# A 256-byte tile for a one-column constant: where the operands of the feed-forward matmuls begin

## The chip, the cores and the metric

The kernel runs on one core of a Trainium2 chip. The metric is the device time of one execution in microseconds (us), median of three runs. Beside the timed runs there is one profiled execution of the kernel; all rows shown here are of that one.

## What is computed

The input is q, k, v of 2 x 8 heads, 768 tokens, head size 64, and two pairs of weights, 512 x 2048 and 2048 x 512. Everything is float32 (the weights arrive as the bits of float64).

```python
# attention, per head: a window of +-15 tokens, and block summaries of 32 tokens
k_sum, v_sum = max over each block of k, mean over each block of v
scores = [q k^T / 8 in the window, q k_sum^T / 8 + log(32)]
x = softmax(scores) @ [v, v_sum]              # -> 1536 tokens x 512
# first network
h = x @ w_in;  g = h - tanh(h);               x = g @ w_out
# second network
h = x @ w_in2; g = h * tanh(softplus(h));     out = g @ w_out2
```

## The kernel before

**Stages.** The attention comes first (some 87 us, units of 128 tokens, loads of keys `kt`, queries `qz` and values beside it), then the two networks. In the last steps of the attention the first blocks of the first network already run.

**The networks.** The 1536 tokens are cut into 3 chunks of 512, d_ff into 16 slices of 128; a step is one network f, one chunk c, one slice i, and there are 2 x 3 x 16 = 96 steps. `ffn_in` (line 489) computes the hidden slice h of a step: 4 pieces of the 512 model columns, each in three matmuls by `mm3` (lines 485 to 487), 12 matmuls of 128 x 128 weights and 512 moving columns. `ffn_out` (line 557) multiplies the gated slice by the slice's output weights into 4 accumulators (`x`, `x`, `tr`, `tr`), again 4 times three matmuls. Three, because every float32 is held as a high and a low part (`xhi`, `xlo`; `ghi`, `glo`; `w[:, 0]`, `w[:, 1]`): high by high, high by low, low by high.

**Operands.** `mm3(out, w, x)` takes `w` as the stationary operand, which a separate load of weights brings in, and `x` as the moving one. In `ffn_in` the weights are a piece of `W[i]` and the moving operand is `xhi` or `xlo`. In `ffn_out` the weights are a piece of `W[i]` and the moving operand is `ghi` or `glo` for the first network (f = 0); for the second (f = 1) `lhs, rhs = (w, g) if f == 0 else (g, w)` exchanges the two. In the rows below the moving operand is named first: `xhi,w`, `ghi,w` and `w,ghi`.

**Order.** It is written out by hand (`tc.manual_schedule()`, the loop from line 628 on): at step n the in-block of step n + 2 is issued, then the out-block of step n - 2. So TensorE's queue holds blocks of 12 matmuls, in and out by turns, with an out-block four slices behind the in-block in front of it; at the end five out-blocks follow one another. Between the two stand the gates: ScalarE and VectorE turn h into `t`, then `ghi` and `glo` (`g_hi`, `g_lo`, lines 503 to 510, two buffers each). The second network's gate takes logarithms, `gate_2n` (line 531), and adds 2 there by a bias column:

```python
    two_c = big.tile([128, 1], F32, name="two_c")             # line 74
        nc.scalar.activation(out=r, in_=n, func=ACTF.Ln, bias=two_c)   # line 537
```

**The weights** are converted from the bits of float64 to the two float32 parts beside everything else, by ScalarE and VectorE (`conv_top`, `conv_or`, `conv_hi`, `conv_lo`), with loads through SyncE's queue.

**Where tiles lie.** Tiles of a pool stand one behind the other in each partition of the on-chip memory, and pools one behind the other, from the left or, with `side="right"`, from the right end. A tile's size is rounded up to 32 bytes. In bytes from the partition's start:

| Tiles | pool | begin at | modulo 256 |
|---|---|---|---|
| xhi0 to xhi2, xlo0 to xlo2, 8192 each | big | 16,512 to 57,472 | 128 |
| w0, w1, w2, 8192 each | big | 65,664, 73,856, 82,048 | 128 |
| two_c, 4 (takes 32) | big | 90,240 | 128 |
| t, ghi, glo, two buffers of 2048 each | tmp | 90,272 to 100,512 | 160 |
| kt0 to kt7, 3328 each; qz0 to qz2, 4096 each | kq (attention only) | 102,560 to 137,376 | 160 |
| w3 to w6, later w7 to w15, 8192 each | wb3, wb7 (kq's place and above) | 102,560 to 200,864 | 160 |

w15 ends at 209,056; on the right, the values, masks, identity and staging buffers begin at fixed places that don't depend on the left side. Within these tiles the operands of the feed-forward matmuls begin at multiples of 512 bytes (weights) or 2048 bytes (moving operand).

Of the kernel before, what the change touches and what calls it, by code (L numbers as in the profile page):

```python
# [9 lines left out]
F32 = mybir.dt.float32  # L10
# [16 lines left out]
def kernel(  # L27
# [7 lines left out]
    w2_d: bass.AP,  # L35
    out: bass.AP,
):
    """qt_d [unit, (e d), hp, 128]: q transposed, head = 2 * hp + e; a unit is 128 tokens.
    kw_d [unit, (e d), hp, 160]: a unit's keys and 16 on either side, transposed; 0 outside the
    sequence.  # L40
    vw_d [unit, 2, 96, h, d]: the values of each half of a unit and 16 on either side.
    vt_d [batch, group, (e d), hp, 256]: v transposed.
    w1_d, w2_d [d_ff / 128, 128, 1024]: the bits of float64 weights, w_in's and w_out's part
    of one slice of d_ff side by side."""
    nc = tc.nc
    NU, _, HP, _ = qt_d.shape
    B, NG = vt_d.shape[:2]
# [15 lines left out]
    big = ctx.enter_context(tc.tile_pool(name="big", bufs=1))  # L63
# [7 lines left out]
    xlo = [big.tile([128, KD, CH], F32R, name=f"xlo{c}") for c in range(NC)]  # L71
    W = {i: big.tile([128, 2, 1024], F32R, name=f"w{i}") for i in range(NPRE)}

    two_c = big.tile([128, 1], F32, name="two_c")
    nc.gpsimd.memset(two_c, 2.0)

    def pst(tag):
        return ps.tile([128, 512], F32, tag=tag, name=tag)

    # The bits of a float64 -> a float32 (its first 24 bits) -> the two float32r parts of that.  # L80
    # The upper 16 bits of a float64, read as a bfloat16 and turned into a float16, are the upper
    # 16 bits of the float32: their exponents' low 3 bits lie in the mantissa, and what lies above
    # loses 112 of its offset, 8 * 112 = 1023 - 127. The middle 32 bits give the rest of the mantissa;
    # they are a word of their own, as the loads land 2 bytes early.
    PW = 256
    IN, OUT = range(0, DM, PW), range(DM, 1024, PW)
    pieces = []
# [6 lines left out]
    def top_tiles(n):  # L94
        tiles = [stg.tile([128, PW], I32, name=f"top{i}") for i in range(n)]
        for t in tiles:
            nc.gpsimd.memset(t, 0)
        return tiles

    def free(n):  # L100
        f, i, o = pieces[n]
        return i in W if f == 0 else (n_in, n_out)[o >= DM] > steps.index((0, NC - 1, i))
# [9 lines left out]
    def conv_top(n):  # L112
        nc.scalar.activation(  # L113
            out=tops[n % len(tops)].bitcast(F16).rearrange("p (n t) -> p n t", t=2)[:, :, 1],
            in_=raws[n].bitcast(BF16).rearrange("p (n t) -> p n t", t=4)[:, :, 2], func=ACTF.Copy,
        )

    def conv_or(n):
        tmps[n] = stg.tile([128, PW], I32, tag="cv", name="cv", bufs=n_cv)
        nc.vector.scalar_tensor_tensor(  # L120
            out=tmps[n], in0=raws.pop(n).bitcast(I32).rearrange("p (n t) -> p n t", t=2)[:, :, 0],
            scalar=13, in1=tops[n % len(tops)], op0=ALU.logical_shift_right, op1=ALU.bitwise_or,
        )

    def conv_hi(n, on_pool):
        f, i, o = pieces[n]
        hi, t = W[i][:, 0, o:o + PW], tmps[n].bitcast(F32)
        if on_pool:
            nc.gpsimd.tensor_copy(hi, t)
        else:  # L130
            nc.scalar.activation(out=hi, in_=t, func=ACTF.Copy)  # L131

    def conv_lo(n, on_pool=False):
        f, i, o = pieces[n]
        ready.add(pieces[n])
        (nc.gpsimd if on_pool else nc.vector).tensor_tensor(  # L136
            out=W[i][:, 1, o:o + PW], in0=tmps.pop(n).bitcast(F32),
            in1=W[i][:, 0, o:o + PW].bitcast(F32), op=ALU.subtract,
        )
# [3 lines left out]
    def conv_ahead(end):  # L143
        nonlocal nl
        while nl < min(n1 + n_raw, end):
            conv_load(nl)
            nl += 1

    def conv_tick(limit, hi_pool=False, lo_pool=False):
        """The first steps of one piece, the middle ones of the one before, the last one of the  # L150
        one before that."""
        nonlocal n0, n1, n2, n3
        while n0 < min(limit, n1 + 2):
            conv_ahead(n0 + 1)
            conv_top(n0)
            n0 += 1
        if n1 < min(n0, n3 + n_cv):
            conv_or(n1)
            n1 += 1
        conv_ahead(limit)  # L160
        if n3 < n2:
            conv_lo(n3, lo_pool)
            n3 += 1
        if n2 < n1 and free(n2):
            conv_hi(n2, hi_pool)
            n2 += 1

    # What shares the attention's work among the engines, by step of the loop below (a step is one
    # unit and parity of heads), or by unit for FILL_DVE
    ASB_DVE = (0, 2, 7, 11, 12, 13, 14, 15, 17, 20, 21)  # L170
    NORM_DVE = (0, 13, 21, 23)
    FILL_DVE = (0, 1, 4, 5, 6, 7, 8, 9, 11)
# [5 lines left out]
    def attention(actx):  # L178
        con = actx.enter_context(tc.tile_pool(name="con", bufs=1, side="right"))
        two = actx.enter_context(tc.tile_pool(name="two", bufs=2, side="right"))  # L180
# [20 lines left out]
        def constants():  # L201
            nonlocal tops
            make_identity(nc, ident)
            k_edges(0)
            for m in range(3):
                nc.gpsimd.memset(masks[m], 0.0)
                for s in range(2):
                    rows = masks[m][T * s:T * s + T]
                    nc.gpsimd.memset(rows[:, SUM[s][0]:SUM[s][1]], math.sqrt(D) * math.log(BLK))
                    reg = rows[:, WND[s][0]:WND[s][1]]  # L210
                    # kept where 1 <= j - i <= 31, and where the key is in the sequence
                    conds = [([[1, KW]], -1, -1), ([[-1, KW]], 2 * WIN - 1, 1)]
                    if (m, s) == (0, 0):
                        conds.append(([[1, KW]], -WIN, 0))
                    if (m, s) == (2, 1):
                        conds.append(([[-1, KW]], KW - WIN - 1, 0))
                    for pattern, base, mul in conds:
                        nc.gpsimd.affine_select(
                            out=reg, in_=reg, pattern=pattern, base=base, channel_multiplier=mul,
                            compare_op=ALU.is_ge, fill=-BIG,  # L220
                        )
            k_edges(UPB)
            tops = top_tiles(2)
# [9 lines left out]
            )  # L233

        def k_edges(u):
            """The 16 keys on either side of the border in front of unit u."""
            l, r = NB, NB + WIN + 128
            if 0 < u < UPB:
                nc.scalar.copy(kt[u][:, :, l:l + WIN], kt[u - 1][:, :, r - WIN:r])
                nc.scalar.copy(kt[u - 1][:, :, r:r + WIN], kt[u][:, :, l + WIN:l + 2 * WIN])  # L240
            elif u == 0:
                nc.gpsimd.memset(kt[0][:, :, l:l + WIN], 0.0)
            else:
                nc.gpsimd.memset(kt[UPB - 1][:, :, r:r + WIN], 0.0)
# [155 lines left out]
        for n in range(3):  # L400
            q_zero(n)
        constants()
        warm = pst("x")
        for n in range(NWARM):
            nc.tensor.matmul(out=warm[:, 0:128], lhsT=ident, rhs=ident, start=n == 0, stop=n == NWARM - 1)
        for u in range(UPB):
            k_sum(u)
            if u:
                k_edges(u)
# [32 lines left out]
        def ticks(j, counts):  # L442
            for _ in range(counts.get(j, 0)):
                conv_tick(len(pieces) // 2, j in HI_POOL, j in LO_POOL)
# [74 lines left out]
        g_hi(z, ts[z])  # L519
        g_lo(z, ts.pop(z))  # L520

    # tanh(softplus(h)) = n / (n + 2), n = u (u + 2), u = exp(min(h, 20)); the reciprocal is
    # exp(-ln(n + 2)) and a Newton step
    def gate_2u(z):
        t = ts[z] = tmp.tile([128, CH], F32, tag="t", name="t")
        nc.scalar.activation(out=t, in_=hs[z], func=ACTF.Exp)
# [63 lines left out]
    steps = [(f, c, i) for f in range(2) for c in range(NC) for i in range(NI)]  # L590
# [31 lines left out]
    with tc.manual_schedule():  # L622
# [5 lines left out]
        for n in range(NS + 2):  # L628
# [17 lines left out]
            if f == 0:  # L646
                more_out(n - 2)
                evac()
                if n == N2 - 1:
                    go(N2, gate_2e)  # L650
                if n:
                    g_hi(z, ts[z])
                if n < N2 - 2:
                    conv_tick(limit)
                if n:
                    g_lo(z, ts.pop(z))
                if n == N2 - 1:
                    go(N2, gate_2f)
                if n < N2 - 2:
                    conv_tick(limit)  # L660
                if n and n + 1 < N2:
                    gate_1(steps[n + 1])
                if n == N2 - 2:
                    nc.scalar.preload_act_table_set("natural_log_exp_and_others")
                    go(N2, gate_2u, gate_2m, gate_2n)
                if n < N2 - 2:
                    conv_tick(limit)
                    conv_tick(limit)
                if n == N2 - 1:
                    go(N2 + 1, gate_2u, gate_2m)  # L670
                continue
# [93 lines left out]
```

## Time and profile before

| | |
|---|---|
| three runs | 619.6, 620.08, 621.63 us; median 620.08 |
| profiled execution: span from the first to the last instruction | 619.7 us |
| TensorE busy (matmul) | 603.5 us, 3212 matmuls |
| VectorE, ScalarE, GpSimd busy | 421.3, 330.4, 53.3 us |
| TensorE's granted clock, mean | 0.997 |

Beside the span the profile gives no further time of that execution. PE is TensorE's matmuls, PEld its loads of weights, DVE VectorE, ACT ScalarE, POOL GpSimd, SP SyncE. Times in rows are in us from the span's start. Matmuls are pipelined: a row's duration (0.39 us) overlaps the next row's, so the distance between two starts tells the pace.

### The profile page before, as it was taken

The numbers are of one execution on the slowest core, as the hardware profiler recorded it, in microseconds if no ns is written. First come the engines' busy times: TensorE is split into PE (matmuls) and PEld (weight loads), VectorE is DVE, ScalarE is ACT, GpSimd is POOL, SyncE is SP. The second block draws the span as 40 slices with busy tenths as digits, with TensorE's granted clock in tenths as the row PEclk, the third lists the DMA queues.
The fourth block names the chain that finished last, engine by engine and source line by source line (L and its number), as shares of the span: only waits on it lengthen the run. The fifth ranks groups of instructions, "written<-read, shape, count | busy, mean of one in ns | idle before, by whom it ended". The sixth has DMA issues, their size and how long they took to land.

```text
span 619.7 us, 9228 instructions
## 1 busy us (share of the span) xinstructions
PE 603.5 (97%) x3212; PEld 493.5 (80%) x3212; DVE 421.3 (68%) x972; ACT 330.4 (53%) x793; POOL 53.3 (9%) x109
## 2 busy tenths in 40 slices
PE   6798999999999999999999999999999999999997
PEld 6587888888888888888888888888888888888886
DVE  6777968877242222367777479997778777597785
ACT  4687868877252112356766456654454444454442
POOL 5545651000000000000000000000000000000000
PEclk9899999999999999999999999999999999999999
DMA  9999547666120000135662101200010000100001
GB/s 232 237 264 255 160 124 249 218 202 190 33 69 17 1 0 1 34 100 150 193 189 68 51 1 51 64 7 1 7 62 1 1 1 0 69 1 1 1 1 68
DMA packets 32302, 52.20 MB, mean 84 GB/s; under 512 B 3392, under 2 KB 25920, under 8 KB 32256
## 3 DMA queue, kind: packets, MB, share of 16 engines
q1 hardware_dynamic: 32256, 51.62, 28.8%
q8 instruction: 25, 0.41, 0.3%
q14 instruction: 21, 0.17, 0.1%
HBM read 48.07 MB, written 3.15 MB: 83 GB/s over the span
## 4 chain that ended last, share of the span: by engine, by line
PE 92%; DMA 6%; SPq 1%; POOL 0%; issue 0%; DVE 0%; POOLq 0%
PE aT L485 7%; PE s L485 7%; PE aT L486 7%; PE s L486 7%; PE aT L487 7%; PE x L485 7%; PE s L487 7%; PE x L486 7%; PE x L487 7%; PE tr L487 7%; PE tr L485 7%; PE tr L486 7%; PE x L368 3%; DMA vtc<-in_vt_dram 2%; PE aT L354 1%; DMA qz<-in_qt_dram 1%
## 5 line engine op out<-in xcount | busy, mean ns | idle before, releaser
L510 DVE TENSOR_TENSOR glo<-t,ghi 128x512 fp32r<-128x512 f32 x48 | 33.4, 696 | 92.3 <-ACT ghi L505 92.2
L505 ACT ACTIVATE ghi<-t 128x512 fp32r<-128x512 f32 x48 | 30.3, 630 | 102.6 <-PE tr L487 102.6
L485 PE MATMUL aT<-xhi,w 128*128 128x512 f32 x192 | 76.1, 396 | 0.0
L485 PE MATMUL s<-xhi,w 128*128 128x512 f32 x192 | 76.0, 396 | 0.0
L486 PE MATMUL aT<-xlo,w 128*128 128x512 f32 x192 | 75.9, 395 | 0.0
L487 PE MATMUL aT<-xhi,w 128*128 128x512 f32 x192 | 75.8, 395 | 0.0
L486 PE MATMUL s<-xlo,w 128*128 128x512 f32 x192 | 75.8, 395 | 0.0
L487 PE MATMUL s<-xhi,w 128*128 128x512 f32 x192 | 75.7, 394 | 0.0
L113 ACT ACTIVATE top<-raw 128x256 f16<-128x256 bf16 x128 | 61.7, 488 | 12.6 <-ACT w L131 5.3
L120 DVE SCALAR_TENSOR_TENSOR cv<-raw,top 128x256 int32<-128x256 int32 x128 | 55.4, 434 | 10.8 <-ACT top L113 7.2
L131 ACT ACTIVATE w<-cv 128x256 fp32r<-128x256 f32 x120 | 47.4, 401 | 9.8 <-DVE cv L120 8.8
L136 DVE TENSOR_TENSOR w<-cv,w 128x256 fp32r<-128x256 f32 x114 | 48.3, 425 | 0.2 <-ACT w L131 0.2
L541 DVE SCALAR_TENSOR_TENSOR t<-n,r 128x512 f32<-128x512 f32 x48 | 33.1, 691 | 20.2 <-ACT r L538 20.1
L510 DVE TENSOR_TENSOR glo<-n,ghi 128x512 fp32r<-128x512 f32 x48 | 33.1, 689 | 16.8 <-ACT ghi L505 16.8
L334 ACT ACTIVATE aa<-aa,neg 128x120 f32<-128x120 f32 x96 | 36.6, 383 | 14.2 <-DVE neg L329 14.2
L505 ACT ACTIVATE ghi<-n 128x512 fp32r<-128x512 f32 x48 | 30.3, 631 | 25.9 <-PE tr L486 18.3
L487 PEld LDWEIGHTS aT<-xhi,w 128*128 128x128 f32 x192 | 36.1, 188 | 8.7
L487 PEld LDWEIGHTS s<-xhi,w 128*128 128x128 f32 x192 | 36.1, 188 | 8.6
L485 PEld LDWEIGHTS aT<-xhi,w 128*128 128x128 f32 x192 | 36.0, 188 | 8.5
L485 PEld LDWEIGHTS s<-xhi,w 128*128 128x128 f32 x192 | 36.0, 188 | 8.5
L486 PEld LDWEIGHTS aT<-xlo,w 128*128 128x128 f32 x192 | 36.1, 188 | 8.3
L486 PEld LDWEIGHTS s<-xlo,w 128*128 128x128 f32 x192 | 36.1, 188 | 8.3
(99 smaller groups left out, 1308.7 us busy)
## 6 DMA issues: line engine op xcount, KB each, us to landing
raw<-in_w_dram SPq DMA_DIRECT2D x128, 255.8 KB, 3.6
vu<-in_vw_dram SPq DMA_DIRECT2D x24, 192.0 KB, 5.9
qz<-in_qt_dram SPq DMA_DIRECT2D x24, 128.0 KB, 6.6
vtc<-in_vt_dram SPq DMA_DIRECT2D x6, 512.0 KB, 7.1
out_dram<-o SPq DMA_DIRECT2D x9, 256.0 KB, 2.1
kt<-in_kw_dram SPq DMA_DIRECT2D x6, 320.0 KB, 5.3
kt<-in_kw_dram SPq DMA_DIRECT2D x6, 256.0 KB, 4.8
out_dram<-t SPq DMA_DIRECT2D x3, 256.0 KB, 2.1
```

Of the source, the lines that this page charges most:

```text
L113: nc.scalar.activation(out=tops[n % len(tops)].bitcast(F16).rearrange("p (n t) -> p n t", t=2)[:, :, 1], in_=raws[n].bitcast(BF16).rearran ...
L120: nc.vector.scalar_tensor_tensor(out=tmps[n], in0=raws.pop(n).bitcast(I32).rearrange("p (n t) -> p n t", t=2)[:, :, 0], scalar=13, in1=top ...
L131: nc.scalar.activation(out=hi, in_=t, func=ACTF.Copy)
L136: (nc.gpsimd if on_pool else nc.vector).tensor_tensor(out=W[i][:, 1, o:o + PW], in0=tmps.pop(n).bitcast(F32), in1=W[i][:, 0, o:o + PW].bit ...
L334: nc.scalar.activation(out=aa[u][:, e, hp, :], in_=aa[u][:, e, hp, :], func=ACTF.Exp, scale=-1.0, bias=neg[u][:, e, hp:hp + 1], accum_out= ...
L368: nc.tensor.matmul(out=xps[u][64 * e:64 * e + 64, hp, T * s:T * s + T], lhsT=vu[u % 3][:, s, 2 * hp + e, :], rhs=asb[u, e][:, hp, T * s:T ...
L485: nc.tensor.matmul(out=out, lhsT=w[0], rhs=x[0], start=first, stop=False)
L486: nc.tensor.matmul(out=out, lhsT=w[0], rhs=x[1], start=False, stop=False)
L487: nc.tensor.matmul(out=out, lhsT=w[1], rhs=x[0], start=False, stop=last)
L505: nc.scalar.activation(out=ghi, in_=t, func=ACTF.Copy)
L510: nc.vector.tensor_tensor(out=glo, in0=t, in1=ghi.bitcast(F32), op=ALU.subtract)
L541: nc.vector.scalar_tensor_tensor(out=ts[z], in0=ns[z], scalar=2.0, in1=rs[z], op0=ALU.add, op1=ALU.mult)
```

## The change

The constant's tile gets 64 columns, of which the first is used. The rest of the diff takes out comments and a docstring and leaves their lines empty, so line numbers stay.

```diff
-    two_c = big.tile([128, 1], F32, name="two_c")
+
+    two_c = big.tile([128, 64], F32, name="two_c")[:, 0:1]
     nc.gpsimd.memset(two_c, 2.0)
```

The tile takes 256 bytes, so what stands behind it on the left begins 224 bytes further on.

## Rows read from the trace of the kernel before

**Rows 1.** The page: busy time, share of the span and instructions of each engine.
```profile
PE 603.5 (97%) x3212; PEld 493.5 (80%) x3212; DVE 421.3 (68%) x972; ACT 330.4 (53%) x793; POOL 53.3 (9%) x109
```

**Rows 2.** The page: chain that ended last, share of the span by engine.
```profile
PE 92%; DMA 6%; SPq 1%; POOL 0%; issue 0%; DVE 0%; POOLq 0%
```

**Rows 3.** Waits of TensorE, whole span: us in total, times, longest (first, last of six).
```profile
PE s L314 <- DMA qz<-in_qt_dram: 5.7, 3, 2.8
...
PE tr L293 <- DVE vsum L280: 0.4, 1, 0.4
```

**Rows 4.** Windows: stretch, us, busy of each engine (instructions), clock, DMA share, GB/s.
```profile
0.00:60.00 60.00, 47.66 (x598) 41.24 (x599) 43.30 (x212) 41.98 (x175) 31.64 (x79) 0.97 0.99 250
97.00:602.11 505.11, 505.11 (x2186) 410.13 (x2185) 337.74 (x648) 254.55 (x517) 0.56 (x2) 1.00 0.20 60
349.50:602.00 252.50, 252.50 (x1093) 205.03 (x1092) 199.80 (x345) 126.61 (x215) 0.00 (x0) 1.00 0.05 16
```

**Rows 5.** Timeline of TensorE, first network: start, duration, line, out<-operands; first matmuls of blocks.
```profile
87.29 0.50 PE L485 MATMUL aT<-xhi,w 128*128 128x512 f32 x1
...
160.93 0.39 PE L485 MATMUL s<-xhi,w 128*128 128x512 f32 x1
...
163.68 0.39 PE L485 MATMUL x<-ghi,w 128*128 128x512 f32 x1
...
171.94 0.39 PE L485 MATMUL aT<-xhi,w 128*128 128x512 f32 x1
...
173.10 0.39 PE L487 MATMUL aT<-xhi,w 128*128 128x512 f32 x1
...
174.46 0.40 PE L487 MATMUL aT<-xhi,w 128*128 128x512 f32 x1
...
182.98 0.40 PE L485 MATMUL s<-xhi,w 128*128 128x512 f32 x1
...
185.79 0.39 PE L485 MATMUL x<-ghi,w 128*128 128x512 f32 x1
...
188.58 0.40 PE L485 MATMUL s<-xhi,w 128*128 128x512 f32 x1
...
202.59 0.39 PE L485 MATMUL x<-ghi,w 128*128 128x512 f32 x1
...
205.33 0.40 PE L485 MATMUL s<-xhi,w 128*128 128x512 f32 x1
```

**Rows 6.** Timeline of TensorE, second network: first matmuls of three blocks in a row.
```profile
538.13 0.40 PE L485 MATMUL s<-xhi,w 128*128 128x512 f32 x1
...
540.93 0.40 PE L485 MATMUL x<-w,ghi 128*128 128x512 f32 x1
...
543.73 0.40 PE L485 MATMUL s<-xhi,w 128*128 128x512 f32 x1
```

**Rows 7.** Timeline of TensorE, the five out-blocks at the end.
```profile
602.11 0.39 PE L485 MATMUL x<-w,ghi 128*128 128x512 f32 x1
...
603.49 0.39 PE L485 MATMUL tr<-w,ghi 128*128 128x512 f32 x1
...
604.85 0.39 PE L485 MATMUL x<-w,ghi 128*128 128x512 f32 x1
...
615.05 0.39 PE L485 MATMUL tr<-w,ghi 128*128 128x512 f32 x1
```

**Rows 8.** The page, costliest groups: busy us, mean ns of one; a load of weights.
```profile
L485 PEld LDWEIGHTS aT<-xhi,w 128*128 128x128 f32 x192 | 36.0, 188 | 8.5
```

**Rows 9.** Waits of all engines, 349.5 to 602 us: ScalarE before it writes ghi.
```profile
ACT ghi L505 <- PE tr L486: 17.6, 28, 0.6
```

**Rows 10.** The page, DMA issues: count, KB each, median us from issue to landing.
```profile
qz<-in_qt_dram SPq DMA_DIRECT2D x24, 128.0 KB, 6.6
...
kt<-in_kw_dram SPq DMA_DIRECT2D x6, 320.0 KB, 5.3
kt<-in_kw_dram SPq DMA_DIRECT2D x6, 256.0 KB, 4.8
```

## The prediction

> **What bounds the kernel now.** I read the page's busy shares first, then the chain of waits, then the table of waits of TensorE, then windows by stage, and last the timeline of single matmuls. TensorE is busy 603.5 us of a span of 619.7 [rows 1], and 92% of the chain that ended last are its instructions [rows 2]. Its waits are six kinds, of which the longest and the shortest stand in [rows 3]; together they make 12.4 us, all at lines of the attention or of its warm-up, none at lines 485 to 487, the three matmuls of the feed-forward layers. [...] Before 60 us it is another kernel: DMA share 0.99, TensorE 47.66 of 60 us [rows 4]. So four fifths of the time are a queue of equal matmuls that never waits for anything, and only the pace of that queue counts there.
>
> A recorded matmul of 0.39 or 0.40 us overlaps its neighbours, so pace has to be read from the distance between starts. The queue alternates between blocks of 12 matmuls: a first-layer block ("in": rows that read xhi and xlo) and a second-layer block ("out": rows that read ghi and glo, four slices behind). Counted back from 602.11, where the last five out blocks begin (slices 11 to 15 of the last chunk), every block has its slice i. Two paces appear:
>
> - in, slices 0 to 2: 160.93 to 163.68, 2.75 us or 229 ns a matmul; out, slice 3: 202.59 to 205.33, 2.74 us, 228 ns [rows 5];
> - in, slice 4: 182.98 to 185.79, 2.81 us, 234 ns; out, slice 0: 185.79 to 188.58, 2.79 us, 233 ns [rows 5]. The second network does the same with the operands' roles exchanged in the out blocks: 538.13, 540.93, 543.73, two times 2.80 us [rows 6].
>
> All blocks from 97.00 to 602.11 follow this: 94 slow ones (76 in with i of 3 and up, 18 out with i under 3) and 88 fast ones (15 in with i under 3, 73 out with i of 3 and up), with [rows 5, 6] as examples of each. So it is neither the slice, nor the layer, nor the network alone. What sorts them is where the two operands start. xhi, xlo and w0 to w2 start 128 bytes past a multiple of 256, ghi, glo and w3 to w15 start 160 past one; every slice taken of them begins a multiple of 256 bytes further on. In-blocks pair 128 with 128 for i under 3 and 128 with 160 above; out-blocks pair 160 with 128 for i under 3 and 160 with 160 above. Equal is fast and unequal slow, in both directions and whichever operand is the moving one.
>
> The fast pace in the mix is not yet the undisturbed one. In the in-block of slice 2 the last six distances, 173.10 to 174.46, take 1.36 us, 226.7 ns each, the first five (171.94 to 173.10) 232 ns [rows 5]. After 602.11 only blocks of 160 with 160 follow: the first six distances take 1.38 us (230 ns), and from 604.85 to 615.05 45 distances take 10.20 us, 226.7 ns, across both accumulator names, four borders between blocks and other ghi and glo buffers [rows 7]. So a run of unequal starts leaves about six matmuls at 230 ns behind it, and an undisturbed equal stream goes at 226.7 ns.
>
> **The change part by part.** The constant itself: one memset on GpSimd writes the same one column, and the 48 activations that use it read it as before; 0 us. Its tile now takes 256 bytes where it took 32. Everything allocated after it from the left moves up by 224 bytes: t, ghi, glo, the keys kt, the queries qz, and w3 to w15. 160 + 224 = 384, which is 128 past a multiple of 256. From then on all feed-forward operands start at 128. No instruction is added, removed or moved in its queue, no wait and no DMA either; the tiles that come from the right side of the memory stay put, and each of w7 to w15 lies over the same attention tiles as before, so no tile has to wait for another one's release than now.
>
> *Pace of the matmuls.* From 97.00 to 602.11 there are 94 + 88 = 182 blocks, 2184 matmuls, in 505.11 us: 231.3 ns each [rows 4]. At 226.7 ns (10.20 us by 45) they take 495.0 us: 10.1 us less. Before 97.00 two in-blocks with i of 3 and 4 save another 24 times 6.7 ns, 0.2 us; after 602.11 six matmuls save 3 ns each, nothing. Sum: 10.3 us. Bounds: if the borders between in and out disturb by themselves, the best that can be had is what slices 0 to 2 show now, where both blocks of a pair are fast: from 160.93 to 171.94 two such pairs take 11.01 us, 5.505 us a pair [rows 5]; 91 pairs take 501.0 us, 4.1 us less. I take the 226.7 ns: within a fast pair the borders still join 128 to 160, because the next load of weights runs beside the last matmul of a block, and it is this that the change removes too; borders between equal blocks after 604.85 disturb nothing [rows 7].
>
> [...]
>
> *What hides the rest.* A load of weights lasts 188 ns [rows 8], under 226.7, so it stays beside the matmul. From 349.5 to 602 us VectorE is busy 199.80 of 252.50 us, ScalarE 126.61 [rows 4]; with 2% less time VectorE goes from 79% to 81%. ScalarE waits there for TensorE before it writes ghi, 28 times, 17.6 us in all [rows 9]: the gate is paced by TensorE, not the reverse. Should one gate step become late, TensorE loses that step's lateness and no more.
>
> *The attention.* kt and qz move together, so matmuls that read both keep their relation; vu, asb, aa and the identity do not move. What does change is where DMAs land: a row of kt began at a multiple of 64 bytes and now begins 32 past one, qz the other way round. No row shows the two for one tile. kt is 6 x 256 + 6 x 320 KB, 3.5 MB, qz 24 x 128 KB, 3.1 MB [rows 10], at 250 GB/s in a stretch that DMA bounds [rows 4]: 14 us and 13 us of queue. If the start counted as much as a factor of two, for both alike, the balance would be 0.4 MB or under 2 us, either way; I take 0, since kt lands in 4.8 to 5.3 us and qz in 6.6 us with half the bytes [rows 10], which their place in the queue explains as well.
>
> 619.7 - 10.3 = 609.4 us of span. The profile gives nothing around the span; it lies 0.4 us under the median of 620.08, so the time comes to 609.8 us.
>
> **The rivals.** *Borders disturb.* The switch between layers costs its six matmuls at 230 ns whatever the addresses: gain 4.1 + 0.2, 615.8 us. For it: no in-block stands next to an equal out-block now, so the trace cannot exclude it. Against it: [rows 7].
>
> *Not the residue but the place.* w0 to w2, xhi and xlo lie together in the lower 90 KB, ghi, glo and w3 to w15 above. A rule "both from the same region" sorts the blocks as well. The change moves all of the upper group by 224 bytes only, so nothing would happen: 620 us. Against it: the border would have to lie just at the constant, between 90,240 and 90,272 bytes, or within the last slice read there, which would be a coincidence. [...]
>
> *Slower: the keys' DMAs.* If a row that begins 32 bytes past a multiple of 64 costs more and qz, for its own reasons (64 partitions), gains nothing back, the start grows by a share of kt's 14 us, before the feed-forward matmuls begin. Above 74% more per byte it eats the 10.3 us; at a factor of two the time is 620.1 + 14 - 10.3 = 623.8 us. For it: DMA bounds the first 60 us [rows 4]. Against it: the queue mixes four streams there, and a part of kt is loaded before anyone waits for it.
>
> **How the numbers follow.** Full pace 0.66 (609.8 us; its own range 608.3 to 611.5, from one 10 ns step of the timeline over 45 distances and the attention's 1 to 2 us); borders disturb 0.19 (613 to 616.8, with cases in between); nothing happens 0.08; slower by the keys 0.04; more gain than forecast 0.03. The range 608.0 to 616.5 takes in the first two. This measurement can tell about 0.3%, 1.9 us, from no change: faster, under 618.2 us, 0.88; the same 0.08; slower 0.04.
>
> **What would show it.** Right: in the timeline all blocks at 2.72 us, also in-blocks of slices 3 to 15, and the distance between two pairs 5.44 us; the windows with TensorE busy throughout from about 97 us and 10 us fewer of them; the attention as long as before. Borders: blocks of 2.74 to 2.76 with six distances at 230 ns after each border. Place: 2.80 and 2.74 as now. Keys: the first feed-forward block later than 87.29 us [rows 5]. The prediction is wrong altogether if equal starts at 128 are slow where now only 160 with 160 was seen (out-blocks), or if TensorE begins to wait for ghi, glo or w.

## The result, and the profile after

The changed kernel takes 610.68 us (median of six runs, 608.96 to 612.7), the kernel before 621.46 us (median of six, 619.6 to 622.92): a ratio of 0.983, interval 0.9812 to 0.9848. The forecast was 609.8 us, faster. The profiled execution took 611.33 us with a span of 609.6 us, so 1.7 us lie around the span.

From line 75 on, lines of the changed kernel are one higher than before (the three matmuls are now 486 to 488); the sentence ahead of the prediction that line numbers stay is wrong by that one line.

The page of the changed kernel, busy times and the chain by engine, which answer to [rows 1, 2]:

```profile
PE 594.0 (97%) x3212; PEld 494.0 (81%) x3212; DVE 421.1 (69%) x972; ACT 330.2 (54%) x793; POOL 53.2 (9%) x109
...
PE 90%; DMA 7%; SPq 1%; DVE 1%; POOL 0%; ACT 0%; issue 0%; POOLq 0%
```

Same instructions, same work on every engine but one: TensorE's matmuls are recorded 9.5 us shorter. Windows of the changed kernel, columns as in [rows 4], the second from the start of the first out-block to the start of the five out-blocks at the end, as there:

```profile
0.00:60.00 60.00, 48.25 (x597) 41.89 (x597) 43.74 (x211) 41.28 (x172) 31.56 (x79) 0.97 0.99 247
...
97.00:592.03 495.03, 495.03 (x2186) 409.90 (x2184) 337.11 (x648) 254.66 (x517) 0.56 (x2) 1.00 0.20 61
```

The same 2186 matmul records took 505.11 us before and take 495.03 us now, 10.08 us less, TensorE busy throughout at the same granted clock of 1.00. After it, 619.7 - 602.11 = 17.6 us were left before and 609.6 - 592.03 = 17.6 us are left now. All of the gain lies in this stretch.

The timeline of the changed kernel: the in-block of slice 2, which the prediction calls the first feed-forward block (those of slices 0 and 1 run before it, from 73.5 us on, inside the attention); in-block of slice 0 and the out-block behind it; slices 4 (in), 0 (out), 5 (in); slices 3 (out) and 8 (in); three blocks of the second network; first and last of the five out-blocks. It answers to [rows 5 to 7].

```profile
87.40 0.50 PE L486 MATMUL aT<-xhi,w 128*128 128x512 f32 x1
...
159.55 0.39 PE L486 MATMUL s<-xhi,w 128*128 128x512 f32 x1
...
162.27 0.39 PE L486 MATMUL x<-ghi,w 128*128 128x512 f32 x1
...
181.31 0.39 PE L486 MATMUL s<-xhi,w 128*128 128x512 f32 x1
...
184.03 0.39 PE L486 MATMUL x<-ghi,w 128*128 128x512 f32 x1
...
186.75 0.39 PE L486 MATMUL s<-xhi,w 128*128 128x512 f32 x1
...
200.35 0.39 PE L486 MATMUL x<-ghi,w 128*128 128x512 f32 x1
...
203.07 0.39 PE L486 MATMUL s<-xhi,w 128*128 128x512 f32 x1
...
442.43 0.39 PE L486 MATMUL s<-xhi,w 128*128 128x512 f32 x1
...
445.15 0.39 PE L486 MATMUL x<-w,ghi 128*128 128x512 f32 x1
...
447.87 0.39 PE L486 MATMUL s<-xhi,w 128*128 128x512 f32 x1
...
592.03 0.39 PE L486 MATMUL x<-w,ghi 128*128 128x512 f32 x1
...
605.40 0.39 PE L488 MATMUL tr<-w,glo 128*128 128x512 f32 x1
```

Every block is 2.72 us, whatever its slice, layer or network: 2.72 / 12 = 226.7 ns. The last 59 distances, 592.03 to 605.40, give 226.6 ns, as [rows 7] did. The blocks that took 2.80 us and those that took 2.75 us are the same now.

TensorE's waits, first and last of the list (us in total, times, longest), and the keys' and queries' loads:

```profile
PE x L369 <- ACT asb L361: 4.7, 4, 2.2
...
PE s L315 <- DVE neg L330: 0.2, 1, 0.2
```
```profile
qz<-in_qt_dram SPq DMA_DIRECT2D x24, 128.0 KB, 6.9
...
kt<-in_kw_dram SPq DMA_DIRECT2D x6, 320.0 KB, 6.4
kt<-in_kw_dram SPq DMA_DIRECT2D x6, 256.0 KB, 4.3
```

None of the five waits is at lines 486 to 488; nothing became late behind the faster matmuls. The loads moved both ways against [rows 10] (kt 5.3 to 6.4 and 4.8 to 4.3, qz 6.6 to 6.9 us), and the in-block of slice 2 starts at 87.40 us where it started at 87.29 us.

### The profile page after: what moved, and what is told of

Read it like the earlier page. It is cut to its first block, busy times and chain, and to the rows that moved or that the text cites. A ratio compares the mean times of both kernels' runs of the same rounds, so it can differ in the third digit from the quotient of the medians.

```text
span 609.6 us, 9228 instructions
## 1 busy us (share of the span) xinstructions
PE 594.0 (97%) x3212; PEld 494.0 (81%) x3212; DVE 421.1 (69%) x972; ACT 330.2 (54%) x793; POOL 53.2 (9%) x109
## 4 chain that ended last, share of the span: by engine, by line
PE 90%; DMA 7%; SPq 1%; DVE 1%; POOL 0%; ACT 0%; issue 0%; POOLq 0%
PE s L486 7%; PE aT L486 7%; PE s L487 7%; PE aT L487 7%; PE s L488 7%; PE tr L487 7%; PE x L487 7%; PE aT L488 7%; PE tr L488 7%; PE x L488 7%; PE tr L486 7%; PE x L486 7%; DMA qz<-in_qt_dram 3%; DMA kt<-in_kw_dram 2%; PE x L369 2%; PE aT L355 1%
## 5 line engine op out<-in xcount | busy, mean ns | idle before, releaser
L486 PE MATMUL s<-xhi,w 128*128 128x512 f32 x192 | 74.9, 390 | 0.0
L486 PE MATMUL aT<-xhi,w 128*128 128x512 f32 x192 | 74.9, 390 | 0.0
L488 PE MATMUL s<-xhi,w 128*128 128x512 f32 x192 | 74.7, 389 | 0.0
L488 PE MATMUL aT<-xhi,w 128*128 128x512 f32 x192 | 74.7, 389 | 0.0
```

The costliest lines, as they stand in the source:

```text
L486: nc.tensor.matmul(out=out, lhsT=w[0], rhs=x[0], start=first, stop=False)
L488: nc.tensor.matmul(out=out, lhsT=w[1], rhs=x[0], start=False, stop=last)
```

## The experiments

All are made from the changed kernel. Each experiment is a single run. The attention's length differs by up to 4 us between them (the in-block of slice 2 starts between 85.20 and 89.31 us), so the second column from the right takes the time from that start to the end of the span, called the feed-forward part below; two in-blocks lie before it.

| Run | starts modulo 256 (x; w0 to w2; ghi, glo; w3 to w15) | us, and the kernel before on the same chip | in-block of slice 2 to end, us | pace seen, ns |
|---|---|---|---|---|
| before | 128; 128; 160; 160 | 621.46 (median) | 532.4 | 233.5 and 229 |
| changed | 128; 128; 128; 128 | 610.68 (median) | 522.2 | 226.7 |
| e1_d64 | 128; 128; 192; 192 | 619.67, 622.6 | 531.7 | 233.3 and 228 |
| e4_all160 | 160; 160; 160; 160 | 613.25, 622.6 | 522.2 | 226.7 |
| e6_w_alone | 128; 128; 160; 128 | 619.0, 622.6 | 532.0 | in 228 to 230, out 233 to 234 |
| e7_g_alone | 128; 128; 128; 160 | 623.96, 622.6 | 535.0 | 233 for slices 3 to 15 |
| e5_map | 128; 128; 128; 128 + 32 (i - 3) | 621.99, 619.27 | 533.2 | 227 to 235 |
| e5b_map16 | the same, + 16 more | 618.6, 619.27 | 531.5 | 227 to 234 |
| e10_u16 | 128; 128; 128; 144 | 614.46, 620.43 | 525.8 | 226.7, later 231 |
| e11_u144 | 128; 128; 128; 16 | 615.58, 620.43 | 527.3 | 226.7, later 233 |
| e12_u16s | 128; 160; 128; 144 | 625.39, 620.43 | 535.4 | 233.3, later 231 |
| e13_u144s | 128; 160; 128; 16 | 625.43, 620.43 | 536.0 | 233, a few in-blocks later 227 |
| e8_half_eq | as changed, 256 columns in in-blocks | 627.68, 619.27 | 539.0 | 119.6 per 256 |
| e9_half_d32 | as before, 256 columns in in-blocks | 625.52, 619.27 | 538.2 | 118.3 per 256, slices 3 to 15 |

**Two halves of the change, another difference, another place.** The theory: the two operands' starts must be equal modulo 256. The rivals: the place as such (lower or upper region), or 128 being a good start. The code shown here and below has added lines only; the lines that they replace and those that set a new tile to 0 are not shown.

```diff
 # e6_w_alone: ghi, glo back to 160, w3 to w15 stay at 128
+    two_c = big.tile([128, 1], F32, name="two_c")[:, 0:1]
+    gap = ctx.enter_context(tc.tile_pool(name="gap", bufs=1)).tile([128, 56], F32, name="gap")
 # e7_g_alone: ghi, glo stay at 128, w3 to w15 back to 160
+    gap = ctx.enter_context(tc.tile_pool(name="gap", bufs=1)).tile([128, 8], F32, name="gap")
 # e1_d64: the constant's tile takes 64 bytes
+    two_c = big.tile([128, 16], F32, name="two_c")[:, 0:1]
 # e4_all160: 32 bytes in front of all
+    lead = big.tile([128, 8], F32, name="lead")
```

> Half of the change: w3 to w15 (and keys and queries) go to 128 modulo 256 by an unused gap of 224 bytes behind ghi and glo, which stay at 160; the constant takes 32 bytes again. Theory: in-blocks of all slices now pair 128 with 128 and are fast (229 to 230 ns, with unequal borders), out-blocks of all slices pair 160 with 128 and are slow (233.5 ns), the five at the end too; 91 slow blocks where the kernel before has 94, so about 620 us, no gain. Rival (the place, lower or upper region): blocks as before, in slow and out fast for slices 3 to 15, also about 620 us. The time does not tell them apart, the blocks do.

> The other half: ghi and glo go to 128 modulo 256 (the constant takes 256 bytes), w3 to w15 with keys and queries go to 160 by an unused gap of 32 bytes in front of them. Theory: in-blocks and out-blocks of slices 3 to 15 both pair 128 with 160 and are slow (233.5 ns), only those of slices 0 to 2 are fast; 149 slow blocks of 182 instead of 94, 55 x 0.055 us = 3 us slower than the kernel before, about 624 us against its 621. Rival (the place): as the kernel before, 621 us.

The timeline of the run with the weights alone (runs with an added tile that is set to 0 have their matmuls at lines 488 to 490): in-block of slice 4, out-block of slice 0, in-block of slice 5; then first and last of the five out-blocks.

```profile
181.00 0.40 PE L488 MATMUL s<-xhi,w 128*128 128x512 f32 x1
...
183.75 0.40 PE L488 MATMUL x<-ghi,w 128*128 128x512 f32 x1
...
186.56 0.40 PE L488 MATMUL s<-xhi,w 128*128 128x512 f32 x1
...
599.33 0.39 PE L488 MATMUL x<-w,ghi 128*128 128x512 f32 x1
...
613.09 0.40 PE L490 MATMUL tr<-w,glo 128*128 128x512 f32 x1
```

The in-block, slow before, is 2.75 us; the five out-blocks at the end, at 226.7 ns in [rows 7], now go at 13.76 / 59 = 233 ns. The timeline of the run with ghi and glo alone, in-block of slice 7, out-block of slice 3, in-block of slice 8:

```profile
199.84 0.39 PE L488 MATMUL aT<-xhi,w 128*128 128x512 f32 x1
...
202.63 0.40 PE L488 MATMUL x<-ghi,w 128*128 128x512 f32 x1
...
205.43 0.40 PE L488 MATMUL s<-xhi,w 128*128 128x512 f32 x1
```

Both blocks take 2.79 to 2.80 us; that out-block took 2.74 us before [rows 5]. Each half moved the slow pace to the blocks that the theory names, and neither half is worth anything alone: 0.4 us less and 2.6 us more than the kernel before in the feed-forward part (expected: about none, and 3 us more). The place alone cannot do this, since w3 to w15 lie in the upper region in both.

> The constant's tile takes 64 bytes: ghi, glo and w3 to w15 begin at 192 modulo 256, xhi, xlo and w0 to w2 at 128, a difference of 64 where the kernel before has 32. Theory (starts have to be equal modulo 256): blocks sort as before, in-blocks of slices 3 to 15 and out-blocks of slices 0 to 2 at about 233.5 ns a matmul, the others at about 229, five out-blocks at the end at 226.7; about 620 us. Rival (only the start modulo 64 counts, 64 being a multiple): every block at 226.7 ns, about 610 us. Rival (the cost grows with the difference): the slow blocks slower than 233.5 ns, and 94 of them times 12 times each further ns make 1.1 us.

> An unused tile of 32 bytes in front of everything, the 256-byte constant kept: all feed-forward operands, keys and queries begin at 160 modulo 256 and none at 128. Theory (equality counts): every block at 226.7 ns, 610 to 611.5 us, as the changed kernel. Rival (128 as such is a good place, or a multiple of 64 or 128 is): all blocks slow at 233 ns or more, 2184 x 6.7 ns over the changed kernel, about 625 us.

Timelines of in-block slice 4, out-block slice 0, in-block slice 5, first with the difference of 64, then with all at 160:

```profile
181.71 0.39 PE L486 MATMUL s<-xhi,w 128*128 128x512 f32 x1
...
184.51 0.40 PE L486 MATMUL x<-ghi,w 128*128 128x512 f32 x1
...
187.31 0.39 PE L486 MATMUL s<-xhi,w 128*128 128x512 f32 x1
```
```profile
183.23 0.39 PE L488 MATMUL s<-xhi,w 128*128 128x512 f32 x1
...
185.95 0.39 PE L488 MATMUL x<-ghi,w 128*128 128x512 f32 x1
...
188.67 0.39 PE L488 MATMUL s<-xhi,w 128*128 128x512 f32 x1
```

A difference of 64 costs what 32 costs (2.80 us), no more, so modulo 64 is out and so is a cost that grows with the distance. With everything at 160 all blocks take 2.72 us and the feed-forward part 522.2 us, the changed kernel's time to a tenth of a microsecond: 128 is nothing special. Starts modulo 512 don't sort the blocks either: by the table of tiles x begins at 128 and w3 to w15 at 384 modulo 512 in the changed kernel, and their in-blocks take 2.72 us.

**Every difference once.** Larger tiles for w3 to w15, each beginning 32 bytes further on modulo 256; in the second run the data begin 16 bytes into the tile.

```diff
+            t = wb.tile([128, 2056], F32R, name=f"w{i}")
+            W[i] = t[:, 0:2048].rearrange("p (t n) -> p t n", t=2)     # e5b_map16: t[:, 4:2052]
```

> The changed kernel with w3 to w15 tiles of 8224 bytes, so that w3 begins at 128 modulo 256, w4 at 160, w5 at 192 and so on in steps of 32; everything else at 128. The difference of the weights to x and to ghi, glo is 0 for slices 0, 1, 2, 3 and 11, 32 times (i - 3) modulo 256 for the others: every multiple of 32 once. Theory (equal modulo 256): in-blocks and out-blocks of slices 0 to 3 and 11 fast (227 to 230 ns a matmul, with unequal neighbours), those of the other eleven slices slow, about 233; some 622 us. Rival (modulo 64): slices 5, 7, 9, 13, 15 fast too. Rival (modulo 128): slices 7 and 15 fast too. Rival (the cost grows with the distance): a slope from slice 4 to slice 10 rather than one level.

> As the run with tiles of 8224 bytes, but the weights' data begin 16 bytes into each tile, so the differences are 16, 48, 80 and so on, odd multiples of 16, for slices 3 to 15, and 0 for slices 0 to 2. Theory (the starts must be equal, to the byte or at least to 16 bytes): all blocks of slices 3 to 15 slow, about 233 ns, 624 us. Rival (units of 32 bytes: 144 to 159 is the place of 128): slices 3 and 11, 16 bytes off, fast. Rival (units of 32 rounded the other way): slice 10, 16 bytes short, fast.

With multiples of 32 the theory holds for nearly every slice: in the first network in-blocks of slices 0 to 3 and 11 take 227.5 to 229.6 ns, slices 7 and 15 (a difference of 128) 232 ns, the others 232 to 234; only slice 9 (192) lies between, at 230. Its out-block in the first network takes 229 ns, which is the equal ones' pace, and in the second network, where the out-blocks exchange the roles, it is slices 5 and 13 (64) whose out-blocks take 230 ns and slice 9's that takes 233 ns. So which operand lies ahead counts too. With odd multiples of 16 it fails. Slices 3 to 15 are not all slow, and the two kinds of block disagree at the same difference. The timeline, in-block of slice 7 (difference 144), out-block of slice 3 (16), the next in-block; then out-block of slice 7 and the next in-block; then in-block of slice 14 (112), out-block of slice 10 (240) and the next in-block:

```profile
197.34 0.39 PE L486 MATMUL aT<-xhi,w 128*128 128x512 f32 x1
...
200.06 0.39 PE L486 MATMUL x<-ghi,w 128*128 128x512 f32 x1
...
202.79 0.39 PE L486 MATMUL s<-xhi,w 128*128 128x512 f32 x1
...
222.24 0.39 PE L486 MATMUL x<-ghi,w 128*128 128x512 f32 x1
...
225.04 0.39 PE L486 MATMUL s<-xhi,w 128*128 128x512 f32 x1
...
236.15 0.40 PE L486 MATMUL aT<-xhi,w 128*128 128x512 f32 x1
...
238.95 0.39 PE L486 MATMUL x<-ghi,w 128*128 128x512 f32 x1
...
241.67 0.39 PE L486 MATMUL aT<-xhi,w 128*128 128x512 f32 x1
```

In-block 7 takes 2.72 us and out-block 3 2.73 us, the fastest there is, with unequal starts; out-block 7, the same weights tile at the same difference, 2.80 us. In-block 7 follows the equal out-block of slice 2, out-block 7 follows an in-block of slice 11 and is followed by slow ones. That suggested a memory: at some differences the queue keeps the pace it arrives with. Out-block 10 shows something more: it takes 2.72 us right behind an in-block of 2.80 us, with unequal starts, so equal starts are not the only ones that make a slow queue fast.

**Memory or not.** One tile for w3 to w6 and one for w7 to w15, the data 16 or 144 bytes in; then the same with w0 to w2 moved to 160, so that slices 0 to 2 are unequal by 32.

```diff
+        t = wb.tile([128, 2048 * n + 64], F32R, name=f"w{len(W)}")
+        for k in range(n):
+            W[len(W)] = t[:, 4 + 2048 * k:4 + 2048 * (k + 1)].rearrange("p (t n) -> p t n", t=2)
 # e11, e13: 36 in place of 4; e12, e13 also:
+    lead = big.tile([128, 8], F32, name="lead")          # in front of w0
+    two_c = big.tile([128, 56], F32, name="two_c")[:, 0:1]
```

> The changed kernel with all weights of slices 3 to 15 at 144 modulo 256, 16 bytes behind x, ghi and glo (w3 to w6 as one tile, w7 to w15 as one, the data 16 bytes in); slices 0 to 2 equal. Theory H (the run with odd multiples of 16: at some differences the queue keeps the pace that it has when it comes there, and equal starts bring it to the fast one): all blocks stay near 226.7 ns, 610 us. Theory D (each difference has its own pace in each kind of block): slices 3 to 15 as slices 3 and 11 of that run, in 233 ns, out 227 in the first and 232 in the second network, about 617 us. Theory E (only equal starts are fast): slices 3 to 15 all at 233 ns, 624 us.

> As the run with 16 bytes everywhere, but w0 to w2 moved to 160 modulo 256 (an unused tile of 32 bytes in front of them), so that slices 0 to 2 are unequal by 32, the slow difference of the kernel before. Theory H: nothing brings the queue to the fast pace any more, slices 3 to 15 stay at about 233 ns too, 625 us. Theory D: slices 3 to 15 as in the run with equal slices 0 to 2. Theory E: all slow, 625 us.

> The same with 144 bytes in place of 16: weights of slices 3 to 15 at 16 modulo 256, the rest at 128. Theory H: 226.7 ns throughout, 610 us. Theory D, as slices 7 and 15 of the run with odd multiples of 16: in 226.7, out 233, about 617 us. Theory E: slices 3 to 15 all at 233 ns, 624 us.

> As the run with 144 bytes everywhere, with w0 to w2 unequal by 32. Theory H: slices 3 to 15 slow, about 625 us. Theory D: slices 3 to 15 as with 144 bytes and equal slices 0 to 2. Theory E: all slow, 625 us.

Starts of in-blocks 13 pairs apart in the first network (312 matmuls) and 4 pairs apart in the second (96 matmuls), 16 bytes behind; first after equal slices 0 to 2, then after slices 0 to 2 unequal by 32:

```profile
175.40 0.39 PE L486 MATMUL aT<-xhi,w 128*128 128x512 f32 x1
...
246.12 0.39 PE L486 MATMUL s<-xhi,w 128*128 128x512 f32 x1
...
487.19 0.39 PE L486 MATMUL s<-xhi,w 128*128 128x512 f32 x1
...
509.35 0.39 PE L486 MATMUL s<-xhi,w 128*128 128x512 f32 x1
```
```profile
179.21 0.40 PE L488 MATMUL aT<-xhi,w 128*128 128x512 f32 x1
...
252.01 0.40 PE L488 MATMUL s<-xhi,w 128*128 128x512 f32 x1
...
497.45 0.40 PE L488 MATMUL s<-xhi,w 128*128 128x512 f32 x1
...
519.62 0.39 PE L488 MATMUL s<-xhi,w 128*128 128x512 f32 x1
```

In the first network 70.72 us against 72.80 us: 226.7 ns against 233.3 ns a matmul. 23 of these 26 blocks have the same difference in both runs (the other three are the out-blocks of slices 0 to 2), and by their starts every single one is at 226.7 ns in the one and 233.3 ns in the other. Only what came before differs. With 144 bytes it is the same (16 pairs of the first network: 226.7 and 233.1 ns). So theory H holds there, in the first network, and D and E fall. In the second network, where the out-blocks exchange the roles and so turn the difference's sign, H fails: both runs take 22.16 and 22.17 us for the four pairs, 230.8 and 230.9 ns, whatever came before, and with 144 bytes 22.35 us each, 232.8 ns. The expected 610 us for the runs after equal slices came out as 614.46 and 615.58 for that reason. The expectation that nothing brings the queue to the fast pace once slices 0 to 2 are unequal missed there too. With 144 bytes and no equal block anywhere, the second network's in-blocks of slices 5 to 7 take 226.7 to 227.5 ns behind out-blocks of slices 0 to 2 at 233 ns; here an out-block of slice 1, in-block of slice 6 and the next out-block:

```profile
460.78 0.40 PE L488 MATMUL x<-w,ghi 128*128 128x512 f32 x1
...
463.58 0.40 PE L488 MATMUL aT<-xhi,w 128*128 128x512 f32 x1
...
466.30 0.40 PE L488 MATMUL x<-w,ghi 128*128 128x512 f32 x1
```

In the first network the same in-blocks, behind out-blocks of the same slices with the difference the other way round, take 233 ns. The pace depends on what came before, but no rule for it was found that holds in both networks.

**One cost per matmul, or per column?** In-blocks as 24 matmuls of 256 columns.

```diff
+        for o in (0, CH // 2):
+            e = o + CH // 2
+            for kk in range(KD):
+                mm3(h[:, o:e], (w[:, 0, kk, :], w[:, 1, kk, :]),
+                    (xhi[c][:, kk, o:e], xlo[c][:, kk, o:e]), kk == 0, kk == KD - 1)
 # e9_half_d32 also:
+    two_c = big.tile([128, 1], F32, name="two_c")[:, 0:1]
```

> The changed kernel (all starts equal), with each in-block as 24 matmuls of 256 moving columns instead of 12 of 512, one half of the columns after the other; the result is the same. It gives the pace of 256 columns at equal starts, to set beside the next run. No theory says how long it is: half of 226.7 ns and up, or the loads of weights (188 ns by their rows) become the bound and the in-blocks take up to 24 x 188 ns = 4.5 us instead of 2.72, 96 times 1.8 us, 780 us in all.

> The same halves with the starts of the kernel before (weights of slices 3 to 15 at 160, x at 128). If the cost of unequal starts is one amount for each matmul with its load, the in-blocks of slices 3 to 15 lose 24 x 6.7 ns = 0.16 us each against the equal halves, 12.5 us in all, and the out-blocks of slices 0 to 2 another 1.1 us. If it is spread over the moving columns, half of that: 0.08 us each, 6.2 us in all. If the loads bound the pace of 256 columns, no difference in the in-blocks, or one of another size.

In-block of slice 4 and the out-block behind it, equal starts, then unequal by 32:

```profile
183.97 0.28 PE L486 MATMUL s<-xhi,w 128*128 128x256 f32 x1
...
186.84 0.40 PE L486 MATMUL x<-ghi,w 128*128 128x512 f32 x1
```
```profile
182.44 0.28 PE L486 MATMUL s<-xhi,w 128*128 128x256 f32 x1
...
185.28 0.39 PE L486 MATMUL x<-ghi,w 128*128 128x512 f32 x1
```

Equal starts take 2.87 us, unequal ones 2.84 us: with 256 columns the sign turns round, by 1.3 ns a matmul. Within the second run it is the same: its equal in-blocks of slices 0 to 2 take 119.6 to 120.0 ns. Both sums expected for the loss, 12.5 and 6.2 us, miss: the cost seen with 512 columns carries over to 256 neither as one amount a matmul nor as one a column. The third expectation, that the loads bound this pace, named no size and stays open. The out-blocks of the first run, equal and with 512 columns, take 229 ns and not 226.7 between such in-blocks. The two runs' feed-forward parts, 539.0 and 538.2 us, are both worse than 522.2.

## Why the prediction was right

*TensorE's pace is the bound.* Busy 505.11 of 505.11 us before [rows 4], four fifths of the span, and 495.03 of 495.03 us now, at a granted clock of 1.00 both times, no wait at its lines: right before and after.

*What sorts the blocks is where the two operands start.* Right for this kernel's starts: the halves of the change moved the slow pace (2.79 to 2.81 us a block) between in- and out-blocks as the sorting says, and the run at 160, with 2.72 us a block, ruled out 128 as such.

*10.1 us from 231.3 to 226.7 ns.* Measured 10.08 us. The 0.2 us forecast for the two in-blocks before 97 us came out as 0.12 (2.89 and 2.80 us before, 2.85 and 2.72 now), and the later start of 0.11 us took it back. The choice that mattered was to take the pace of [rows 7], not that of the fast blocks in the mix, which would have given 4.1 us. The reason given was that mixed borders and not the switch between layers spoil the fast blocks. The changed kernel shows that the switch does not: every block there, with its border, takes 226.7 ns a matmul. The trace of before has the next load of weights beside the last matmul of a block: ahead of the block at 163.68 us a load of 0.19 us begins at 163.45, beside a matmul of 0.40 us from 163.44 on. That this load was what spoiled the fast blocks is argued and not shown.

*The rivals.* Borders: fell by the changed kernel's blocks of 2.72 us. Place: fell by the halves. The keys' loads: 0.11 us at the in-block of slice 2, within what runs differ by.

*The time.* The span was forecast at 609.4 and is 609.6 us. What lies around it was taken as 0.4 us from the median of three runs; the profiled execution has 1.7 us. By its size 611.1 us would have been the forecast, and 610.68 was measured. How close the forecast came in the time, 0.9 us, is partly luck: the six runs spread over 3.7 us.

*Too wide.* "Equal is fast and unequal slow" was the reading of two differences, 0 and 32. Unequal starts of 16 and 144 bytes run at 226.7 ns too in the first network when the queue comes from a fast stretch; that the six matmuls at 230 ns after an unequal stretch are a trace of the same memory is likely and not shown. Equal starts brought the queue towards 226.7 ns from a slow stretch in every run with 512 columns throughout (227 to 231 ns a matmul), but so did some unequal ones: 240 bytes in the out-block of slice 10 (226.7 ns), and 144 in the second network's in-blocks (226.7 to 227.5 ns). Why starts count was not seen; only starts, distances and their order were.

## What to carry to other kernels

Where TensorE is the bound and nothing waits, read the distance between starts of matmuls block by block, and sort the blocks by the addresses of both operands before looking for another cause; an undisturbed stretch, here the five blocks at the end at 226.7 ns a matmul, showed the pace that was then had throughout. For streams of 512-column float32r matmuls give weights and moving operands the same start modulo 256 bytes, all of them: all equal took 2.72 us a block of 12, a difference of 32 bytes 2.80 us, and either half alone gained nothing (0.4 us less and 2.6 us more in the feed-forward part). This was seen with all at 128 and with all at 160. With other column counts measure it anew, since at 256 columns equal starts took 119.6 ns and unequal ones 118.3.

## What the runs showed of the hardware that was not expected

- A row of 312 matmuls, 276 of them at the same differences of starts, ran at 226.7 or at 233.3 ns throughout, depending on slices 0 to 2.
- A difference of 64 bytes cost the same as 32 (233.3 ns a matmul, 2.80 us a block), and 128 nearly the same (232 ns); 192 cost less in the first network (229 to 230 ns).
- 256 columns: 119.6 ns with equal and 118.3 ns with unequal starts. In the changed kernel every matmul has its load of weights (3212 of each), recorded at 188 ns in the in-blocks. If a load takes as long at 256 columns, loads followed one another faster than their recorded time; whether they bound the pace is open.
